# Wider spacing between wo's loads and their splits, and scratch matmuls among seven of v's products

## The chip, the core and the metric

The kernel runs on one core of a Trainium2 chip. The metric is the device time of one execution in microseconds (us). The core has five engines that work through their own queues and wait for each other by semaphores: TensorE (PE, matrix products, with its weight loads shown apart as PEld), VectorE (DVE), ScalarE (ACT), GpSimd (POOL) and SyncE (SP, which here issues DMA transfers). A kernel is compared with another by the medians of several runs.

## The reference

The input x has 2048 rows of 512. Two branches work on it and are mixed by a gate per row. The reference, cut to what is computed:

```python
def _A_ref(x, wq, wk, wv, wo):              # 32 heads of 16, one k and one v for all
    q = (x @ wq).reshape(B, S, H, Dh).transpose(0, 2, 1, 3)
    k, v = x @ wk, x @ wv
    p = softmax(einsum("bhqd,bkd->bhqk", q, k) * Dh ** -0.5)
    o = einsum("bhqk,bkd->bhqd", p, v)
    return o.transpose(0, 2, 1, 3).reshape(B, S, H * Dh) @ wo

def _B_ref(x, w1, b1, w2, b2):              # 512 -> 1792 -> 512
    h = relu(x @ w1 + b1)
    return (h * h) @ w2 + b2

g = sigmoid((x * gate_w).sum(-1, keepdims=True))
return g * _A_ref(x, ...) + (1 - g) * _B_ref(x, ...)
```

## The kernel before

**Precision.** The larger products (those of q, the dense branch and the output) run on numbers that are split in two: a rounded part r and the rest l = value - r. Each product is then three matmuls (r with r, r with l, l with r). `split` makes the two parts on DVE: a CAST (line 192) and a subtraction (line 193). The weights wo are split once, in four quarters, into wor and wol.

**Attention.** The 32 heads and four chunks of 512 query rows make 32 iterations. In each, 32 steps u (units of key tile and half chunk) run through: scores on PE (line 763) go either into the two-bank tiles s, from which ACT takes the exponential straight into e (line 800), or into the single bank x, which DVE copies to e first (line 784, COPY e<-x), so that ACT takes the exponential there. Then PE multiplies e with v into the accumulator acc (line 814, the context, groups of 16 or 24 matmuls in the profile). At an iteration's end the accumulator is copied, repacked by DMA (oc, lc) and divided on DVE (lines 833 to 840). The bank x is one only: PE's next score in x waits for DVE's copy of the one before.

**Other matmuls.** Between the scores of a block stand the twelve-matmul units of the projections of q, the dense branch and the output projection. They come from the generator `work` and accumulate in the banks mm (line 1107). Every 32 x 512 block of scores and its unit of matmuls form a "phase", followed by a context block.

**The order of the work.** It is laid out by a planner in the kernel's own Python. It keeps estimated times of the engines, at_pe, at_act and at_dve. Work of DVE that has no fixed place stands in lists: `soon`, `divisions`, `chores`. `spend` takes from them whatever fits until the given estimated time, divisions ahead of chores, chores in order. A chore that loads something returns a number of microseconds, and `held` is then set to that much after the present estimate: the next chore that computes is placed no earlier. The number is LANDS (6.0) or DIVIDES (10.0) us. The tile `stage` takes what is loaded so: its first half serves the chores (wo here, later x and the attention's output), its other two quarters belong to the loads of w1 and w2. wo is loaded in two transfers of two quarters each (line 943), and each transfer is followed in `chores` by two splits.

**The start.** v comes as sixteen small products of 17 columns (`v_tiles`, line 336) out of kvc, into a bank vp that is later called acc. After each of the first nine stands a scratch matmul (line 339) into columns of the same bank that nobody reads: 240 columns wide, with the constant ones as weights. The last seven stand behind the first scores; behind them come a tiny copy named peek (line 1208), which makes DVE pass a finished bank, the copies of v and z (`v_rows`, lines 343 and 344) and a row of k_aug (`k_shift`, line 330).

**SP's queue** issues, in order, the loads of weights (line 474), of wo (943), of b2 (1033), the writes and reads of q's parts in DRAM (355, 420, 434) and the repacking (204, 205). A transfer that waits holds up those behind it.

Of the kernel before, what the change touches and what calls it, by code (L numbers as in the profile page):

```python
# [32 lines left out]
ROOT = float(0x1fbd1df5 + 0x80000)  # L33
WARM = 10
PARTS = [slice(a, min(a + 86, CH)) for a in range(0, CH, 86)]
LANDS, DIVIDES, SURE = 6.0, 10.0, 0.7
PAIR, CONTEXT, TURN, EXP, COPY, LATE = 0.235, 0.429, 0.36, 0.925, 0.66, 0.3
GROUPS = (0, 1, 2, 3), (4, 5, 6, 7), (8, 9, 10), (11, 12, 13)
AHEAD = 4
# [124 lines left out]
def mix_kernel(ctx: ExitStack, tc: tile.TileContext, xT, wkv, wq, wo, w12, b1, b2, cst, out):  # L164
# [63 lines left out]
    with fast, tc.tile_pool(name="at", bufs=1) as at, \  # L228
# [103 lines left out]
        def v_tiles(tiles, vp, idle=0):  # L332

            for i in tiles:
                c, j = divmod(i, 4)
                nc.tensor.matmul(vp[:, i * 17:i * 17 + 17], kvc[:, c, j * 128:(j + 1) * 128],
                                 cs[:, C_SEL:C_SEL + 17], start=True, stop=True)
                for _ in range(idle):
                    nc.tensor.matmul(vp[:, 272:], ones, sqk[:, 0, 272:], start=True, stop=True)

        def v_rows(vp):
            vz = vp[:, :16 * 17].rearrange("p (i d) -> p i d", i=16)
            nc.vector.tensor_copy(v_ext[:, :, 0:32:2], vz[:, :, :DH])
            nc.vector.tensor_copy(z, vz[:, :, DH])
# [96 lines left out]
        def stage():  # L441

            if not staged:
                staged.append(keep.tile(sh, F32, name="stage", tag="r2"))
            return staged[0]
# [136 lines left out]
        vp = ap.tile([128, CH], F32, name="acc")  # L582
# [26 lines left out]
        def later(f, *args):  # L609
            chores.append((1.2, lambda: f(*args)))  # L610
# [326 lines left out]
        def o_ready(c):  # L937

            if c == 0 and not wos:
                wos.extend(xp.tile(sh, F32R, name=n, tag=t) for n, t in (("wor", "xr2"), ("wol", "xl2")))  # L940

                def load(a):
                    nc.sync.dma_start(stage()[:, :2], wo[a * 256:a * 256 + 256].rearrange("(t p) n -> p t n", p=128))
                    return LANDS

                for t in range(KT):
                    if t % 2 == 0:
                        chores.append((0.0, lambda t=t: load(t // 2)))
                    later(split, wos[0][:, t], wos[1][:, t], stage()[:, t % 2])
            if c > 0:  # L950
                ask(c - 1)

        def ask(c, n=KT):
            if c in asked or any((c, t) not in complete for t in range(n)) or c > len(asked):
                return
            if c and not used[c - 1]:
                return
            asked.add(c)
            tiles = []

            def load(a):
                if a == 0:
                    tiles.extend((keep.tile(sh, F32R, name="orr", tag="r3"), xp.tile(sh, F32R, name="orl", tag="xl3")))
                m = min(2, n - 2 * a)
                i = c * NG + 4 * a
                nc.sync.dma_start(stage()[:, :m], oTs[i:i + 2 * m].rearrange("(t u) d n -> (u d) t n", u=2))
                return DIVIDES

            def part(t):
                orr, orl = tiles  # L970
                split(orr[:, t], orl[:, t], stage()[:, t % 2])
                if t == n - 1:
                    osp[c] = orr, orl

            for t in range(n):
                if t % 2 == 0:
                    chores.append((0.0, lambda t=t: load(t // 2)))
                later(part, t)
# [228 lines left out]
        phase(span.slots, AHEAD + 2, 0)  # L1207
        nc.vector.tensor_copy(at.tile([128, 1], F32, name="peek"), span.bank[:, :1])
        evicted = True
        v_tiles(range(9, 16), vp)  # L1210
        v_rows(vp)
        k_shift(1)
        dve(1.6, at_pe + 2.2)
# [72 lines left out]
```

## Time and profile before

| | |
|---|---|
| median of 3 runs | 1226.75 us (1225.81 to 1229.14) |
| profiled execution | 1228.71 us, of which its span 1227.0 us |
| mean granted TensorE clock | 0.994 |
| busy: PE, ACT, DVE, weight loads, POOL | 99%, 84%, 63%, 55%, 5% of the span |
| the chain of waits by line | PE acc L814 37%, PE mm L1107 33%, PE s L763 17%, PE x L763 6% |

The span is the time from the first to the last instruction of the profiled execution. The granted clock is the share of full speed that TensorE's throttle allowed. A busy share says how long an engine had work, not that it set the time; the chain of waits is followed back from the last instruction to what released each step, and says whose work the end hung on. Idle time of PE shows in the timeline in brackets, with what ended it.

### The profile page before, as it was taken

The page shows a single profiled execution, that of the slowest core. Times are in us where ns is not written, and L with a number is a line of the kernel's source. Part 1 is how long each engine was busy: PE and PEld are TensorE (multiplying, and loading weights), DVE is VectorE, ACT ScalarE, POOL GpSimd, SP SyncE. Part 2 cuts the span into 40 slices and gives each one's busy share as a digit, 9 for nine tenths or more (in the row PEclk, how much of TensorE's full clock was granted, in tenths as well). Part 3 has the DMA queues.
Part 4 walks back from the last instruction along what each step waited for, and adds up shares of the span by engine and source line. Part 5 has one row for each costly group of instructions (what it writes and reads, how often), then busy time and mean ns, then how long its engine had stood idle before and what let it go on. Part 6 is the DMA issues. An engine that isn't in the chain of part 4 may idle for free.

```text
span 1227.0 us, 24104 instructions
## 1 busy us (share of the span) xinstructions
PE 1211.2 (99%) x9839; PEld 673.4 (55%) x9839; DVE 771.2 (63%) x1516; ACT 1035.5 (84%) x1146; POOL 66.3 (5%) x87
## 2 busy tenths in 40 slices
PE   9999989999999999999999999999999999999997
PEld 4555545555555555555555555555555555555553
DVE  5765768466576864837678574655848476663643
ACT  6788868888988888888888888988888888988875
POOL 1001020000000200000002001000010000001000
PEclk9999989999999999999999999999999999999999
DMA  6344331121113223112133122112132222113011
GB/s 227 78 120 117 102 88 49 48 75 40 52 57 120 88 74 91 53 32 66 57 100 117 57 61 92 49 40 74 38 91 64 57 67 81 36 31 91 23 52 37
DMA packets 45347, 88.71 MB, mean 72 GB/s; under 512 B 10642, under 2 KB 10898, under 8 KB 44720
## 3 DMA queue, kind: packets, MB, share of 16 engines
q1 hardware_dynamic: 37024, 68.27, 18.7%
q0 software_dynamic: 8064, 18.59, 4.9%
q8 instruction: 79, 1.29, 0.5%
q14 instruction: 36, 0.29, 0.1%
q10 hardware_dynamic: 144, 0.26, 0.1%
HBM read 57.83 MB, written 20.97 MB: 64 GB/s over the span
## 4 chain that ended last, share of the span: by engine, by line
PE 93%; DVE 2%; ACT 2%; DMA 1%; SPq 1%; issue 1%; DVEq 0%; ACTq 0%
PE acc L814 37%; PE mm L1107 33%; PE s L763 17%; PE x L763 6%; ACT e L800 1%; DVE e L784 1%; SPq L420 1%; DMA stage<-in_wo 0%; DMA xf<-in_xT 0%; PE mm L296 0%; PE mm L200 0%; DVE qr L392 0%; DVE ql L393 0%; PE s L306 0%; DVE ot L1249 0%
## 5 line engine op out<-in xcount | busy, mean ns | idle before, releaser
L800 ACT ACTIVATE e<-s 128x1024 f32<-128x1024 f32 x822 | 781.7, 1026 | 165.9 <-PE s L763 165.3
L784 DVE COPY e<-x 128x512 f32<-128x512 f32 x404 | 279.1, 691 | 389.1 <-PE x L763 354.1
L814 PE MATMUL acc<-e,v_ext 128*32 128x512 f32 (+1 forms) x4224 | 484.3, 586 | 0.0
L763 PE MATMUL s<-qa,k_aug 49*128 49x512 f32 x1644 | 462.4, 413 | 0.2
L763 PEld LDWEIGHTS s<-qa,k_aug 49*128 49x128 f32 x1644 | 234.8, 185 | 75.0 <-ACT e L800 54.0
L814 PEld LDWEIGHTS acc<-e,v_ext 128*32 128x32 f32 x4224 | 116.1, 109 | 241.9 <-issue 238.2
L1107 PE MATMUL mm<-w2r,hr 64*128 64x512 f32 x896 | 229.2, 402 | 0.0
L800 ACT ACTIVATE e<-e 128x1024 f32<-128x1024 f32 x202 | 214.7, 1063 | 0.8 <-DVE e L784 0.8
L763 PE MATMUL x<-qa,k_aug 49*128 49x512 f32 x404 | 164.7, 408 | 5.4 <-DVE e L784 4.2
L1107 PEld LDWEIGHTS mm<-w2r,hr 64*128 64x128 f32 x896 | 135.7, 186 | 45.9 <-DVE hr L193 9.2
L1107 PE MATMUL mm<-w2l,hr 64*128 64x512 f32 x448 | 143.9, 392 | 0.0
L763 PEld LDWEIGHTS x<-qa,k_aug 49*128 49x128 f32 x404 | 75.1, 186 | 51.3 <-DVE w2l L491 12.6
L1107 PEld LDWEIGHTS mm<-w2l,hr 64*128 64x128 f32 x448 | 80.5, 186 | 6.9
L1107 PE MATMUL mm<-xragain,w1r 64*128 64x512 f32 x224 | 76.3, 418 | 0.2
L1107 PE MATMUL mm<-xr,w1r 64*128 64x512 f32 x224 | 74.3, 416 | 0.0
L1107 PE MATMUL mm<-xlagain,w1r 64*128 64x512 f32 x224 | 74.0, 391 | 0.0
L1107 PE MATMUL mm<-xragain,w1l 64*128 64x512 f32 x224 | 73.1, 392 | 0.0
L1107 PE MATMUL mm<-xl,w1r 64*128 64x512 f32 x224 | 72.4, 391 | 0.0
L1107 PE MATMUL mm<-xr,w1l 64*128 64x512 f32 x224 | 72.0, 395 | 0.0
L839 DVE RECIPROCAL n<-n 128x86 f32<-128x86 f32 x90 | 61.5, 683 | 1.8
L1107 PEld LDWEIGHTS mm<-xragain,w1r 64*128 64x128 f32 x224 | 38.2, 185 | 27.7 <-issue 9.2
L1107 PEld LDWEIGHTS mm<-xr,w1r 64*128 64x128 f32 x224 | 37.9, 185 | 26.8 <-issue 8.4
(162 smaller groups left out, 1181.4 us busy)
## 6 DMA issues: line engine op xcount, KB each, us to landing
stage<-in_w SPq DMA_DIRECT2D x56, 256.0 KB
qa<-qs SPq DMA_DIRECT2D x186, 64.0 KB
w1f<-in_w SPq DMA_DIRECT2D x28, 256.0 KB
w2f<-in_w SPq DMA_DIRECT2D x28, 256.0 KB
qs<-qr SPq DMA_DIRECT2D x16, 256.0 KB
ress<-res POOLq DMA_DIRECT2D x4, 1024.0 KB, 5.1
qs<-ql POOLq DMA_DIRECT2D x15, 256.0 KB, 7.5
oc<-accs SPq DMA_DIRECT2D x30, 128.0 KB
```

The costliest lines, as they stand in the source:

```text
L420: nc.sync.dma_start(bass.AP(tensor=o.tensor, offset=o.offset, ap=[[KS * 2 * CH, 4], [CH, 2], [1, CH]]), nrm[32 * i:32 * i + 8].bitcast(F32))
L763: nc.tensor.matmul(dst.rearrange("p (a n) -> p a n", a=2), k_aug[rows, kt * 128:(kt + 1) * 128], qa[it][rows, :, q * HC:q * HC + HC], star ...
L784: nc.vector.tensor_copy(e_half(u)[:, 2 * r:2 * r + 2], x.rearrange("p (a n) -> p a n", a=2))
L800: nc.scalar.activation(e_half(u), src, AF.Exp, scale=SCALE)
L814: nc.tensor.matmul(acc[h * 32:(h + 1) * 32, cols], v_ext[:, kt], es[u // 2][:, h % 2 * 2 + h // 2, mine], start=(kt == 0), stop=(kt == NK ...
L839: return ((0.23, bound), (0.35, compare), (0.72, lambda: nc.vector.reciprocal(n[0], n[0])), (0.28, lambda: nc.vector.tensor_tensor(o[:, co ...
L1107: nc.tensor.matmul((self.before if r else self).bank, a[p], b[p], start=not r and i == 0, stop=r == 1 and i == len(self.terms[1]) - 1, ski ...
```

## The change

A new constant, WRITES = 14.0, is what a load of wo returns in place of LANDS = 6.0. And the last seven products of v get one scratch matmul each, as the first nine have. They are 240 columns wide; the constant ones is their weight.

```diff
-LANDS, DIVIDES, SURE = 6.0, 10.0, 0.7
+LANDS, DIVIDES, WRITES, SURE = 6.0, 10.0, 14.0, 0.7
...
                 def load(a):
                     nc.sync.dma_start(stage()[:, :2], wo[a * 256:a * 256 + 256].rearrange("(t p) n -> p t n", p=128))
-                    return LANDS
+                    return WRITES
...
         evicted = True
-        v_tiles(range(9, 16), vp)
+        v_tiles(range(9, 16), vp, 1)
         v_rows(vp)
         k_shift(1)
```

The first number moves instructions on DVE and on SP's queue. PE's, ACT's and POOL's orders stay as they are but for the scratch matmuls.

On DVE, around the first two splits of wo, at 168.56 and 170.24 us of the profile, the order before is:

```order
L784 COPY e<-x 128x2x256
L491 TENSOR_TENSOR w1l<-stage,w1r 128x512
L784 COPY e<-x 128x2x256
L192 CAST wor<-stage 128x512
L193 TENSOR_TENSOR wol<-stage,wor 128x512
L784 COPY e_1883<-x 128x2x256
L192 CAST wor<-stage 128x512
L193 TENSOR_TENSOR wol<-stage,wor 128x512
L784 COPY e_1883<-x 128x2x256
L662 TENSOR_SCALAR big<-mm,b1t 128x512
```

The same place of DVE now:

```order
L784 COPY e<-x 128x2x256
L784 COPY e_1888<-x 128x2x256 x2
L662 TENSOR_SCALAR big<-mm,b1t 128x512
L663 TENSOR_TENSOR big<-big 128x512
L192 CAST hr<-big 128x512
L193 TENSOR_TENSOR hr<-big,hr 128x512
L784 COPY e<-x 128x2x256 x2
L482 CAST w1r<-w1f 128x512
L491 TENSOR_TENSOR w1l<-w1f,w1r 128x512
L784 COPY e<-x 128x2x256
L192 CAST wor<-stage 128x512
L193 TENSOR_TENSOR wol<-stage,wor 128x512
```

The two pairs CAST and TENSOR_TENSOR on wo have left this place; the first pair of the new order stands where the third stood before (181.18 us), the second where the fourth stood (190.00 us).

The third and fourth pairs now stand on DVE behind the divisions of the next finished pair of iterations, which before ended at 216.00 us:

```order
L839 RECIPROCAL n<-n 128x82
L784 COPY e<-x 128x2x256
L840 TENSOR_TENSOR oc<-oc,n 128x82
L192 CAST wor<-stage 128x512
L193 TENSOR_TENSOR wol<-stage,wor 128x512
L784 COPY e<-x 128x2x256
L686 SCALAR_TENSOR_TENSOR res_2133<-mm,omg,res_2133 128x512
L192 CAST wor<-stage 128x512
L193 TENSOR_TENSOR wol<-stage,wor 128x512
```

Before, there was no work on wo at this place; the other rows stood in the same order.

On SP's queue the second load of wo moves behind eleven transfers (a load of w1, the two of the repacking, eight of q for the next iteration):

```order
 L474 DMA stage<-in_w 128x512
+L474 DMA w1f<-in_w 128x512
+L204 DMA oc<-accs 64x512
+L205 DMA lc<-accs 64x512
+L434 DMA qa<-qs 16x1024 x3
+L434 DMA qa<-qs 1x1024
+L434 DMA qa<-qs 16x1024 x3
+L434 DMA qa<-qs 1x1024
 L943 DMA stage<-in_wo 128x2x512
-L474 DMA w1f<-in_w 128x512
```

The first load keeps its place.

On PE, among the last seven products of v:

```order
 L763 MATMUL s<-qa,k_aug 128x512 x2
-L336 MATMUL acc<-cs,kvc 128x17 x7
+L336 MATMUL acc<-cs,kvc 128x17
+L339 LDWEIGHTS ones
+L339 MATMUL acc<-sqk,ones 128x240
+L336 MATMUL acc<-cs,kvc 128x17
```

The last three rows repeat until there are seven products and seven scratch matmuls.

## The prediction

> **What bounds the kernel now.** I read the page's chain of waits first, to learn which engine sets the end.
>
> ```profile
> PE 93%; DVE 2%; ACT 2%; DMA 1%; SPq 1%; issue 1%; DVEq 0%; ACTq 0%
> ```
>
> TensorE (PE) carries 93% of the chain, so a microsecond counts only if PE loses it. I then listed the granted clock in half-microsecond stretches over the whole span. Apart from the last four microseconds, after PE's work, it is below full in only two places, around 32 to 36 us and 168 to 176 us. The windows view over both places (length, then busy us and, in brackets, instructions of PE, its weight loads, DVE, ACT and POOL, then the granted clock, the DMA share and GB/s):
>
> ```profile
> 21.96:25.38 3.42, 3.34 (x31) 2.83 (x30) 2.80 (x8) 3.00 (x6) 0.00 (x0) 1.00 0.44 99
> ...
> 28.79:32.20 3.41, 3.41 (x25) 2.46 (x21) 2.65 (x7) 3.02 (x4) 0.00 (x0) 1.00 0.17 60
> 32.20:35.61 3.41, 3.26 (x17) 2.60 (x18) 3.27 (x10) 2.99 (x3) 0.00 (x0) 0.50 0.74 231
> ...
> 165.25:168.66 3.41, 1.68 (x15) 1.03 (x11) 0.10 (x1) 1.96 (x2) 0.00 (x0) 1.00 0.83 304
> 168.66:172.07 3.41, 1.70 (x9) 0.96 (x13) 3.34 (x7) 0.00 (x0) 2.66 (x2) 0.51 0.04 11
> 172.07:175.49 3.42, 3.42 (x16) 0.47 (x16) 2.75 (x4) 1.97 (x2) 3.42 (x3) 0.50 0.59 153
> ```
>
> The clock is halved for 3.41 us and later for 6.83 us, twice that; and from 35.61 to 168.66 there are 39 times 3.41 us. So in this trace the clock is set anew every 3.41 us on a fixed beat: a stretch in which PE did too little is followed by one at half speed. Each part of the change stands in the stretch ahead of one of these two drops. The timeline (start, duration, engine, operation; in brackets the idle time before it and what ended it) shows the second place on VectorE (DVE) and PE:
>
> ```profile
> 168.56 0.43 DVE L192 CAST wor<-stage 128x512 fp32r<-128x512 f32 x1 [5.34 <-DMA stage<-in_wo]
> ...
> 169.63 0.68 DVE L784 COPY e<-x 128x512 f32<-128x512 f32 x1
> ```
>
> ```profile
> 162.96 1.92 PE L814 MATMUL acc<-e,v_ext 128*32 128x512 f32 x16
> ...
> 170.37 0.79 PE L763 MATMUL x<-qa,k_aug 49*128 49x512 f32 x1 [3.44 <-DVE e L784]
> ...
> 171.95 3.64 PE L814 MATMUL acc<-e,v_ext 128*32 128x512 f32 x16
> 175.52 0.52 PE L1107 MATMUL mm<-xr,w1r 64*128 64x512 f32 x2
> ...
> 178.12 1.92 PE L814 MATMUL acc<-e,v_ext 128*32 128x512 f32 x16
> ```
>
> DVE stands 5.34 us at the first split of wo, whose load has not landed. The copy of scores behind it, which empties the one bank x, is late, and PE, which needs x, stands 3.44 us. Then PE works at half clock until 175.5 us: the same sixteen context matmuls take 3.64 us there and 1.92 elsewhere. The chain of waits, in order of time, gives the landing, and the starts of undisturbed context blocks:
>
> ```profile
> 163.31 5.24 DMA stage<-in_wo
> ...
> 178.17 1.87 PE acc L814 x16
> 182.58 1.85 PE acc L814 x16
> 187.00 1.85 PE acc L814 x16
> ```
>
> **The change part by part.** First, the splits. The order shows no change in PE's, ACT's or POOL's work from here on. On DVE, two pairs leave the place of 168.56 and 170.24; the next two places, which served the second load, now serve the first; and two new places follow behind the divisions. What the first load then meets:
>
> ```profile
> 181.18 0.42 DVE L192 CAST wor<-stage 128x512 fp32r<-128x512 f32 x1
> ```
>
> Without the stall this place is reached some 6.3 us sooner, at about 174.9 us, and the load lands at 163.31 + 5.24 = 168.55: 6.3 us to spare. If PE is also earlier by the second part below, so is the load's issue, which follows PE and DVE. What that saves: from the context block at 162.96 to the one at 178.12 are 15.16 us for two periods (each sixteen context matmuls, two x products, six s products and twelve of the unit). Undisturbed periods of this form take 182.58 - 178.17 = 4.41 and 187.00 - 182.58 = 4.42 us. So the loss here is 15.16 - 8.83 = **6.3 us**: 3.44 of standing, half of the 5.15 us from 170.37 to 175.52 for the clock, and 0.3 around them. Its lower bound is 3.44 us, if the clock dropped all the same.
>
> The second load moves on SP's queue (the DMA queue of SyncE) from its old place ahead of the second row here to one ahead of the last, behind eleven others:
>
> ```profile
> 156.59 6.68 SPq L420 DMA_DIRECT2D qs<-nrm  x4
> ...
> 179.75 0.33 SPq L474 DMA_DIRECT2D w1f<-in_w  x1
> ...
> 191.01 3.38 SPq L434 DMA_DIRECT2D qa<-qs  x8
> 194.48 0.35 SPq L474 DMA_DIRECT2D stage<-in_w  x1
> ```
>
> It is issued where the last row stands, less the 7.5 us by which all is earlier here: about 187 us, and lands, by the first load's 5.24, near 192. The weights' load of the last row goes out 0.4 us later behind it; its reader comes 12 us after the issue, which hides that:
>
> ```profile
> 206.93 0.63 ACT L496 ACTIVATE w1r<-stage 128x512 fp32r<-128x512 f32 x1
> ```
>
> The new places of the splits are behind the rows of 216.00 and 219.07 on DVE:
>
> ```profile
> 216.00 0.23 DVE L840 TENSOR_TENSOR oc<-oc,n 128x82 f32<-128x82 f32 x1
> 218.47 0.69 DVE L784 COPY e<-x 128x512 f32<-128x512 f32 x1 [2.23 <-PE x L763]
> 219.07 0.74 DVE L686 SCALAR_TENSOR_TENSOR res<-mm,omg,res 128x512 f32<-128x512 f32 x1
> 222.60 0.69 DVE L784 COPY e<-x 128x512 f32<-128x512 f32 x1 [2.79 <-PE x L763]
> ```
>
> They come up near 208.7 and 212.3 us, over 16 us behind the landing. A pair takes 169.63 - 168.56 = 1.07 us and falls into DVE's idle 2.23 and 2.79 us: no cost. Without that cover each would hold up a copy of x, 1.1 us apiece. The finished halves of wo are first read much later, so nobody else waits for them:
>
> ```profile
> L1107 PE MATMUL mm<-wor,orr x120: 385/394/502, 459.8 to 1203.5; 64*128 64x512 f32 x120
> ```
>
> Second, the scratch matmuls. Seven products of v are now each followed by a matmul of 240 columns, as the first nine were already:
>
> ```profile
> 24.50 0.30 PE L336 MATMUL acc<-cs,kvc 128*128 128x17 f32 x2
> ...
> 24.75 0.30 PE L336 MATMUL acc<-cs,kvc 128*128 128x17 f32 x2
> ...
> 29.82 1.74 PE L336 MATMUL acc<-cs,kvc 128*128 128x17 f32 x14
> ```
>
> With scratch a product takes 24.75 - 24.50 = 0.25 us. Without, fourteen halves take 1.74 us, of which the last 0.26 is one duration: 1.48 / 13 x 2 = 0.23. So seven scratch matmuls add 7 x 0.02 and the last one's end, 0.25 us together. PE then has a wait that covers it:
>
> ```profile
> 32.16 0.15 DVE L1208 COPY peek<-mm 128x1 f32<-128x1 f32 x1
> ...
> 32.36 0.28 PEld L1107 LDWEIGHTS mm<-xr,wqr 64*128 64x128 f32 x1 [0.59 <-DVE peek L1208]
> ...
> 32.74 0.87 DVE L330 TENSOR_SCALAR k_aug<-km 1x512 fp32r<-1x512 f32 x2
> ...
> 33.24 1.01 ACT L800 ACTIVATE e<-s 128x1024 f32<-128x1024 f32 x1
> ...
> 36.28 0.39 PE L1107 MATMUL mm<-xr,wql 64*128 64x512 f32 x1
> 36.51 0.39 PE L1107 MATMUL mm<-xr,wqr 64*128 64x512 f32 x1
> ...
> 37.52 2.78 PE L814 MATMUL acc<-e,v_ext 128*32 128x512 f32 x24
> ```
>
> The peek does not depend on v, so PE goes on at 32.37 as before; 0.25 us is the price if that wait were gone. Does the clock hold? The stretch 21.96 to 25.38 held all nine products with scratch and was followed by full clock; the stretch 28.79 to 32.20 held the seven bare ones, with PE busy throughout by the page, and was followed by half. In the new order the latter gets 7 x 240 columns more, so I take it that the clock holds. What that is worth: PE's steps after 32.37 at full clock come every 0.23 us (36.28 to 36.51). Three steps, and the score pair stands at about 33.1; but its second half needs the shifted row of k_aug, ready at 32.74 + 0.87 = 33.61, so PE leaves it at 33.7, where it is today. Three steps and a score pair: 34.6. Three steps: 35.3; the next score pair needs the bank that ACT frees with the end of the activation after that of 33.24, 33.24 + 2 x 1.01 = 35.3: no wait to speak of. The pair and three steps, and context begins near 36.3 instead of 37.52: **1.2 us**. The bounds are nothing (the clock drops anyway) and half of the 3.41 us, 1.7.
>
> [...]
>
> **The sum** is made against the profiled execution, 1228.71 us (its span 1227.0, and 1.7 around it): 1228.71 - 6.3 - 1.2 = **1221.2 us**. That execution is 1.96 above the median 1226.75, and the runs go from 1225.81 to 1229.14. I read the spread as the fixed beat falling elsewhere: were a stretch to begin just ahead of PE's standing, one half-clock stretch would follow, not two, and at the first place perhaps none. With the drops gone the new kernel should have little of this spread, so I put its median at 1221.2, and not at 1226.75 - 7.5 = 1219.2, which stays the lower bound. To 1226.75 that is -5.5 us, 0.45%.
>
> **The rivals.**
>
> The clock falls at 32 us regardless, because what counts is the wait for the peek or a measure of work that 240 columns do not reach. For it: the beat's place differs by run. Against: the stretch 21.96 to 25.38. [...] Price: the second term lost, 1222.4.
>
> The wait moves rather than goes: the first split still waits, or a split on its new place holds a copy of x. For it: SP's queue took 6.68 us for four small issues (qs<-nrm) just ahead of the first load, and may take longer. Against: 6.3 and 16 us to spare. Half a stall, say 2 us of standing and a half-clock stretch of 3.41 us (1.7): 1225.
>
> Slower: the second load stays stuck behind the eight loads of q and the third split stands. It holds DVE, x and so PE, as at 168.56. It costs from the point at which the load lands after 208.7 us, against 192 expected. It decides once the new kernel loses 1230.4 - 1221.2 = 9.2 us (0.3% above the old median), that is 6.6 us of standing and 2.6 of half clock: a landing past 215.3 us; at 216 the time is 1231. The hold-up of 6.7 us in the SP rows above is what speaks for it; 23 us of it is far off.
>
> **How the numbers follow.** Forecast 0.79, own range 1219.2 to 1222.2; clock falls anyway 0.10; wait moves 0.08; slower 0.03. The measurement tells about 0.3%, 3.7 us, from no change: faster means below 1223.1. The forecast and the first rival lie below it, 0.89 together, the wait that moves lies within, and the slower case is above. The range for 8 in 10 takes in the lower bound with 0.4 us beneath it for the runs' own scatter, and the first rival with half of the second: 1218.8 to 1224.0.
>
> **What would show it.** On the changed kernel's timeline, no idle time ahead of a split of wo; x at about 165.7 us copied by DVE without delay; context blocks 4.4 us apart through 160 to 180; the granted clock 1.00 in all stretches until PE's last work; context first at 36.3. A clock of 0.5 at 32 refutes the second term; a DVE row on wor released by stage<-in_wo refutes the first. If both are as said and the time is above 1223, something outside these two places took it back.

## The result and the profile after

| | before | changed |
|---|---|---|
| median, runs beside each other | 1226.38 us (1225.09 to 1229.14, 7 runs) | 1221.62 us (1220.89 to 1222.54, 7 runs) |
| profiled execution, and its span | 1228.71 us, 1227.0 us | 1221.62 us, 1219.9 us |
| mean granted TensorE clock | 0.994 | 0.999 |

The ratio is 0.9952, with a 95% interval of 0.9937 to 0.9966: the changed kernel is faster by 0.48%. The forecast was 1221.2 us.

The page of the changed kernel, the chain of waits by engine:

```profile
PE 94%; DVE 2%; ACT 2%; DMA 1%; issue 1%; SPq 0%; ACTq 0%; DVEq 0%
```

PE carries a little more of a shorter chain (94% against 93%), so part of what went was time in which PE did not work; work at half clock counts as PE's share all the same (3.57 us of acc at 172.02 in the chain of before, against 1.85 to 1.87 for a block at full clock). The windows view of the changed kernel over two stretches of its own beat at the start, and over the place of the old stall (window, its length, then busy us and instructions of PE, its weight loads, DVE, ACT and POOL, granted clock, DMA share, GB/s):

```profile
29.19:32.60 3.41, 3.41 (x30) 2.59 (x30) 2.80 (x8) 2.94 (x5) 0.00 (x0) 1.00 0.15 54
32.60:36.01 3.41, 3.35 (x29) 2.32 (x25) 3.03 (x7) 3.41 (x5) 0.00 (x0) 1.00 0.75 246
160.00:167.00 7.00, 7.00 (x60) 3.63 (x60) 3.87 (x6) 6.43 (x7) 1.10 (x1) 1.00 0.44 153
167.00:176.00 9.00, 9.00 (x76) 4.61 (x72) 7.57 (x13) 7.70 (x9) 5.40 (x4) 1.00 0.10 29
```

Both drops of the clock are gone, and PE is busy for all 16 us of 160 to 176. (The edges of the beat are counted back in steps of 3.413 us from the drop behind PE's last work. The step is measured in before: 307 of them lie between the end of the half clock at 175.59 us and the drop at 1223.48, and 39 between 35.64 and 168.76.) The timeline of the changed kernel on DVE, where the four splits of wo stand now:

```profile
164.13 0.69 DVE L784 COPY e<-x 128x512 f32<-128x512 f32 x1 [1.83 <-PE x L763]
...
173.81 0.42 DVE L192 CAST wor<-stage 128x512 fp32r<-128x512 f32 x1
...
182.62 0.42 DVE L192 CAST wor<-stage 128x512 fp32r<-128x512 f32 x1
...
208.75 0.42 DVE L192 CAST wor<-stage 128x512 fp32r<-128x512 f32 x1
...
212.33 0.42 DVE L192 CAST wor<-stage 128x512 fp32r<-128x512 f32 x1
```

No split has a bracket, so none waits; the copy of x waits for PE, and no longer the other way round. On PE, the first context block, and those through the old stall:

```profile
36.28 1.92 PE L814 MATMUL acc<-e,v_ext 128*32 128x512 f32 x16
...
161.74 1.92 PE L814 MATMUL acc<-e,v_ext 128*32 128x512 f32 x16
...
166.14 1.92 PE L814 MATMUL acc<-e,v_ext 128*32 128x512 f32 x16
...
170.75 1.92 PE L814 MATMUL acc<-e,v_ext 128*32 128x512 f32 x16
```

They are 4.40 and 4.61 us apart, at 1.92 us each: 9.01 us for the two periods that took 15.16. And SP's queue in the changed kernel:

```profile
153.39 3.85 SPq L420 DMA_DIRECT2D qs<-nrm  x4
157.29 0.44 SPq L943 DMA_DIRECT2D stage<-in_wo  x1
...
183.63 3.38 SPq L434 DMA_DIRECT2D qa<-qs  x8
187.10 0.39 SPq L943 DMA_DIRECT2D stage<-in_wo  x1
```

The first load goes out 6 us sooner than in the profile of before; only 1.2 us of that is the lead that all had by then.

Where the 7.1 us between the two spans lie is read from the starts of context blocks in both traces, before less changed: 1.24 us at the first (37.52 and 36.28), 1.22 at the block of 82.92 and 81.70, 0.87 at the next, 1.22 again at 162.96 and 161.74, 7.37 behind the old stall (178.12 and 170.75), 7.10 at the end. The 0.35 us at 87 us is a wait that is new on DVE:

```profile
83.86 0.43 DVE L482 CAST w1r<-w1f 128x512 fp32r<-128x512 f32 x1 [1.27 <-DMA w1f<-in_w]
```

Its load was issued at 80.58, behind q's eight loads, against 79.40 before. Three more steps of about 0.3 us, at 267, 464 and 659 us, are given back by 958 us. They stand in the profiles of after_again, after_more, narrow32, long_peek, writes10, filled_stall and only_scratch too, and not in those of only_writes and before_2, which lack the seven scratch matmuls. act_queue, which has them, shows the step at 267 and little of the other two. What makes the steps is not known.

### The profile page after: what moved, and what is told of

Its sections match the earlier page's. It is cut to its first block, busy times and chain, and to the rows that moved or that the text cites. A ratio compares the mean times of both kernels' runs of the same rounds, so it can differ in the third digit from the quotient of the medians.

```text
span 1219.9 us, 24119 instructions
## 1 busy us (share of the span) xinstructions
PE 1207.6 (99%) x9845; PEld 669.9 (55%) x9846; DVE 771.5 (63%) x1516; ACT 1035.1 (85%) x1146; POOL 64.8 (5%) x87
## 4 chain that ended last, share of the span: by engine, by line
PE 94%; DVE 2%; ACT 2%; DMA 1%; issue 1%; SPq 0%; ACTq 0%; DVEq 0%
PE acc L814 37%; PE mm L1107 33%; PE s L763 17%; PE x L763 6%; ACT e L800 2%; DVE e L784 1%; DMA xf<-in_xT 0%; PE mm L296 0%; PE mm L200 0%; DMA w1f<-in_w 0%; DVE qr L392 0%; DVE ql L393 0%; PE s L306 0%; DVE ot L1249 0%; PE x L881 0%
```

## The experiments

Four questions: does each part do what it was credited with; why was the load late; what makes the clock fall; and where do the runs of the kernel before get their spread. None of the kernels leaves out work of the reference.

### Each part alone, and the change once more

only_writes takes the scratch matmuls out of the changed kernel:

```diff
-        v_tiles(range(9, 16), vp, 1)
+        v_tiles(range(9, 16), vp)
```

> The wider spacing of wo alone, v's last seven products bare. Theory (two separate losses, of which the stall of DVE and PE at the first split is one): no wait on stage<-in_wo, context blocks 4.4 us apart at 160 to 180 us, the clock at 0.5 for one stretch of 3.4 us near 32 us, first context block near 37.5 us; median 1222.4 to 1223.0. Rival (the scratch matmuls did nothing, all of the gain is the spacing's): 1221.6.

Measured: 1222.62 us (1221.81 to 1226.59, 11 runs), ratio 0.9975 (0.9961 to 0.9989). The windows view of only_writes over two stretches of its beat:

```profile
29.61:33.02 3.41, 3.22 (x25) 2.61 (x25) 2.62 (x8) 2.94 (x4) 0.00 (x0) 1.00 0.25 66
33.02:36.43 3.41, 3.41 (x19) 2.85 (x17) 2.57 (x5) 3.02 (x4) 0.00 (x0) 0.50 0.72 243
```

The drop at the start is there, the first context at 37.46, and no split waits. The splits' part alone does what was said of it.

only_scratch takes the splits' part out:

```diff
-                    return WRITES
+                    return LANDS
```

> The seven scratch matmuls alone, wo's splits where they were. Theory: first context block near 36.3 us, full clock there; the first split of wo waits 3 to 5 us and the clock falls after it; median 1225.2, 1.2 below before. Rival 1 (scratch did nothing): 1226.4. Rival 2 (the earlier start lets SP's queue issue wo's load sooner, as it did in the changed kernel, 157.3 against 163.3 us, so the stall shrinks by itself): 1221.6 to 1223.

Measured: 1227.48 us (1223.47 to 1232.08, 12 runs), ratio 0.9998 (0.9981 to 1.0015), some 2 us above what was expected. The first context stands at 36.38, so the start was repaired. The stall took that back. DVE's timeline in only_scratch, and then the step of its chain of waits behind it:

```profile
168.50 0.43 DVE L192 CAST wor<-stage 128x512 fp32r<-128x512 f32 x1 [5.87 <-DMA stage<-in_wo]
```

```profile
159.24 9.24 DMA stage<-in_wo
```

The load went out 4.1 us sooner than in the profile of before (163.31) and landed at the same 168.5, after 9.24 us in place of 5.24. The lead of 1.1 us at the start was lost in the longer wait. As a measure of the scratch alone this run is inconclusive: the stall's own spread is wider than 1.2 us.

after_again is the changed kernel without any edit, run beside these.

> The changed kernel once more, beside the two halves on the same chip. 1221.6, with a profile whose context blocks start within 0.4 us of the first profile's; where they differ, in steps of 0.3 us, the steps are scatter and not the change's.

Measured: 1221.38 us (1220.99 to 1221.93, 6 runs), ratio 0.9952 (0.9938 to 0.9966). Less only_writes, 1222.62, that prices the scratch at 1.24 us.

### Why the load was late

act_queue keeps the splits where they were before and sends wo's loads through ScalarE's queue (the scratch matmuls stay):

```diff
-                    nc.sync.dma_start(stage()[:, :2], wo[a * 256:a * 256 + 256].rearrange("(t p) n -> p t n", p=128))
-                    return WRITES
+                    nc.scalar.dma_start(stage()[:, :2], wo[a * 256:a * 256 + 256].rearrange("(t p) n -> p t n", p=128))
+                    return LANDS
```

> The scratch matmuls, wo's splits where they were before (6.0 us of spacing), but wo's two loads are issued from ACT's queue instead of SP's. Theory A (the load was late because it stood behind q's small writes on SP's queue, 6.7 us): it goes out some 5 us sooner, lands before the split's place, no stall, 1221.3 to 1222.3. Theory B (6.0 us is too short for the transfer itself, wherever it is issued): DVE waits 2 to 5 us again, 1224 to 1225.5.

Measured: 1221.85 us (1220.68 to 1222.68, 6 runs), ratio 0.9953 (0.9938 to 0.9968). The timeline of act_queue: the load's issue on ScalarE's queue, and the first split.

```profile
155.45 0.42 ACTq L943 DMA_DIRECT2D stage<-in_wo  x1
```

```profile
163.23 0.42 DVE L192 CAST wor<-stage 128x512 fp32r<-128x512 f32 x1
```

The split is at its old place and waits for nothing: the load was there by 163.23. It went out 0.93 us ahead of SP's first issue of qs<-nrm, which stands at 156.38 in this trace. So the load was late because of what stood ahead of it in SP's queue, and spacing the splits is one of two cures that are equal within the scatter.

The traces in which a split waits say more. In each, the start of the four qs<-nrm (the timeline of SP), the load's issue, and its landing (from the chain of waits; in filled_stall, from the split that it releases):

| | q's eight loads | qs<-nrm begins | wo issued | wo landed | from qs<-nrm |
|---|---|---|---|---|---|
| before | 7.87 us | 156.59 | 163.31 | 168.55 | 11.96 |
| before_2 | 6.59 us | 155.74 | 159.88 | 167.97 | 12.23 |
| only_scratch | 7.21 us | 156.23 | 159.24 | 168.48 | 12.25 |
| filled_stall (below) | 5.32 us | 153.21 | 157.00 | 165.6 | 12.4 |
| writes10 (next) | 8.38 us | 156.34 | 162.18 | 167.72 | 11.38 |
| before_3 (below) | 7.38 us | 161.56 | 164.59 | 174.01 | 12.45 |
| only_scratch_2 (below) | 7.80 us | 161.19 | 167.93 | 173.28 | 12.09 |

The issue moves by 3.7 us (3.01 to 6.74) against the start of the writes (2.96 to 6.69 us of them) and the landing hardly: the load comes about 12 us after the first of the four writes, however soon it is issued behind them. The hold-up is thus not the queue's issuing alone. It fits a load that stands behind the writes' data, but that was not tried by itself. A lack of bandwidth does not fit in before_2: the DMA share, taken each half microsecond from 165.0 to 167.5, was 0.24 to 0.31, while the load was still out (it landed at 167.97). In before it was 0.80 to 1.04 from 165 to 168, with the load out until 168.55, so there it is not ruled out. And the writes in turn begin 0.8 to 1.4 us after q's eight loads ahead of them have been issued. The timeline of SP in filled_stall, where those took 5.32 us:

```profile
146.54 5.32 SPq L434 DMA_DIRECT2D qa<-qs  x8
...
153.21 3.74 SPq L420 DMA_DIRECT2D qs<-nrm  x4
157.00 0.44 SPq L951 DMA_DIRECT2D stage<-in_wo  x1
```

In before they took 7.87 us from 147.74 on. So in these traces the landing is spread, against PE's work, mostly by how long SP is busy with q's loads, two steps ahead.

writes10 sets the constant to 10.0, between the two:

```diff
-LANDS, DIVIDES, WRITES, SURE = 6.0, 10.0, 14.0, 0.7
+LANDS, DIVIDES, WRITES, SURE = 6.0, 10.0, 10.0, 0.7
```

> The changed kernel with 10.0 in place of 14.0: the first split stands one copy later than before, some 2.5 us on in time, and the third ahead of one place less. Theory (the stall is as long as the load lands after the split's place): with landings seen between 162 and 168.5 us the wait is 2.5 us shorter and often gone, median 1221.5 to 1223.5, the scatter between that of before and that of the changed kernel. Rival (any place past the planner's 6 us will do): 1221.4, no scatter.

Measured: 1223.93 us (1222.12 to 1228.74, 12 runs), ratio 0.9977 (0.9963 to 0.9991), some 0.4 us above what the theory expected and far from the rival's. The timeline of writes10, DVE and then PE:

```profile
167.74 0.43 DVE L192 CAST wor<-stage 128x512 fp32r<-128x512 f32 x1 [2.59 <-DMA stage<-in_wo]
```

```profile
170.21 0.50 PE L1107 MATMUL mm<-xr,w1r 64*128 64x512 f32 x2 [1.82 <-DVE big L662]
...
173.10 0.50 PE L763 MATMUL x<-qa,k_aug 49*128 49x512 f32 x1 [0.53 <-DVE e L784]
```

The split waits 2.59 us, half of what it did, and what stands behind it on DVE is late: first line 662, which empties a bank mm that PE waits 1.82 us for, then a copy of x, 0.53 us. The clock does not fall: the context blocks at 173.76 and 178.14 take 1.92 us each, and the mean clock of this execution is 0.999. The gain follows the spacing: some 2 to 2.5 us are still lost at 10 (against 1221.38 and 1221.93 for the unedited kernel, run beside other experiments), none at 14.

### What the stall costs beside the wait

filled_stall keeps the old places and puts fourteen matmuls of 512 columns on PE where it stands, into a bank of s that is overwritten afterwards (LANDS in place of WRITES, as in only_scratch, and this, which the first split of wo sets off):

```diff
+                for _ in range(fill.pop()):
+                    nc.tensor.matmul(parts[u + 1][0][:, 0], cs[:, :64].bitcast(BF), cs[:, :CH // 2].bitcast(BF),
+                                     start=True, stop=True)
             score(u, r, x)
```

> Scratch among v's products, wo's splits at their old place, and 14 scratch matmuls of 512 columns (3.0 us) on PE ahead of the product x that waits in the stall: the wait stays, the clock should not fall. Theory (of the stall's 6.3 us, 3.4 are standing and 2.6 the half clock behind it): full clock at 165 to 180 us, and from the block ahead of the wait to the one after the next 8.8 us plus the standing alone, some 12.3 instead of 15.2; median 2 to 2.6 below the scratch alone, 1224 to 1225.5. Rival (the loss is the standing and its backlog on DVE, the clock is by the way): as the scratch alone, 1227.

Measured: 1225.84 us (1224.79 to 1231.04, 12 runs), ratio 0.9991 (0.9974 to 1.0007). The timeline of filled_stall, DVE and then PE:

```profile
165.59 0.43 DVE L192 CAST wor<-stage 128x512 fp32r<-128x512 f32 x1 [3.47 <-DMA stage<-in_wo]
```

```profile
165.47 3.19 PE L786 MATMUL s<-cs 128*128 128x512 bf16 x13
...
168.59 0.50 PE L763 MATMUL x<-qa,k_aug 49*128 49x512 f32 x1
```

PE has work through the wait and the clock stays at full: the context blocks behind it, at 169.49 and 174.08, take 1.92 us each. The median is 1.6 us under that of only_scratch, 2 to 2.6 were expected, and the two ranges and the intervals of the two ratios overlap: the direction is as the theory has it, but by the times alone it is not clear of the noise. The clock is: 11 of the 12 runs have a mean clock of 0.998 or more, against 4 of only_scratch's 12. (Its single wait of 3.47 us is no measure of the edit: the writes began 3 us earlier in this execution.) So PE at work through this stall kept the clock (0.999 over the profiled execution); the wait stayed.

### What makes the clock fall at the start

narrow32 makes the seven scratch matmuls 32 columns wide (`v_tiles` passes the width on to line 339):

```diff
-        v_tiles(range(9, 16), vp, 1)
+        v_tiles(range(9, 16), vp, 1, 32)
```

> The changed kernel, with the seven new scratch matmuls cut from 240 to 32 columns. Theory (the clock is set by the columns that PE streams in a stretch of 3.4 us): 32 columns are too little, the clock is at 0.5 for one stretch near 32 to 36 us, first context block near 37.4 us, median 1222.4 to 1222.8, as with bare products. Rival (any further matmul between the products holds the clock, whatever its width): clock 1.00, context near 36.4, 1221.4.

Measured: 1222.28 us (1221.65 to 1223.92, 9 runs), ratio 0.9962 (0.9946 to 0.9978). In the profiled execution the clock stays full and the first context stands at 36.47, against what was expected. The median lies between that of the changed kernel and that of only_writes. The runs beside the profiled one differ from it: the four at a mean clock of 0.999 go from 1221.65 to 1222.17 us, the five at 0.998 or less from 1222.28 to 1223.92. Of only_writes' 11 runs ten are at 0.998 or less, of the changed kernel's 25 (counted further down) one. So by the mean clock 32 columns hold it in some runs and not in others.

long_peek puts a reduction, estimated at 0.7 us, on DVE ahead of the peek, which makes PE's wait longer (0.93 us against 0.35), with all of the change in place:

```diff
         phase(span.slots, AHEAD + 2, 0)
+        nc.vector.tensor_reduce(at.tile([128, 1], F32, name="slow"), span.bank, AX.X, OP.max)
         nc.vector.tensor_copy(at.tile([128, 1], F32, name="peek"), span.bank[:, :1])
```

> The changed kernel with one more reduction of 0.7 us on DVE ahead of the peek, so that PE waits there about 1.0 us instead of 0.35, longer than the 0.59 of the kernel before. Theory (thin matmuls set off the drop, not this wait): full clock, first context block 0.3 to 0.7 us later than in the changed kernel, 1221.7 to 1222.1. Rival (the wait for the peek sets it off): 0.5 for 3.4 us, context 1.5 us and more later, 1222.9 or above.

Measured: 1222.13 us (1221.41 to 1226.46, 8 runs), ratio 0.9963 (0.9943 to 0.9982). The timeline of PE's weight loads in long_peek shows the longer wait, and the windows view what followed:

```profile
33.24 0.18 PEld L1107 LDWEIGHTS mm<-xr,wqr 64*128 64x128 f32 x1 [0.93 <-DVE peek L1209]
```

```profile
30.22:33.64 3.42, 2.92 (x28) 2.32 (x30) 2.68 (x8) 2.94 (x5) 0.00 (x0) 1.00 0.27 77
33.64:37.05 3.41, 3.41 (x20) 2.67 (x18) 2.96 (x6) 2.15 (x3) 0.00 (x0) 0.50 0.75 226
```

With scratch in place and a wait of 0.93 us the drop is back in this execution: 1.00 becomes 0.50 at the edge of the beat behind it. It is not so in most runs: six of the eight have a mean clock of 0.999 or more and lie from 1221.41 to 1222.74 us, about where the theory had them. So with the longer wait the drop comes in some runs only, by the mean clock; that the beat's place is the reason is the author's guess, which no run shows.

### Where the spread of the runs comes from

The experiments up to here suggested that the landing of the load alone, and not the beat, might spread the runs of the kernel before. Two more profiled executions of that kernel (before_2, before_3), and one more of only_scratch (only_scratch_2), were to tell the two apart.

> The kernel before once more, for where its scatter comes from. Theory A: the landing of wo's first load sets it, through SP's queue and the transfer; the profiled time then follows the idle time that the trace shows ahead of the first split of wo: 5.34 us of it went with 1228.71, and each microsecond less of idle time should take 1 to 1.4 us off, down to 1222.6 with no idle time. Theory B (the prediction's): the fixed beat of the clock falls elsewhere; then the idle time ahead of the split is again 5 to 5.6 us, and the time differs by the number of half-clock stretches, 1.7 us each.

> A third look at the kernel before. Theory A: time and idle time ahead of the first split of wo move together as in the run beside it. Theory B: the idle time stays at 5 to 5.6 us and the time follows the number of half-clock stretches.

> The kernel with the scratch matmuls alone, once more. Theory A: its profiled time is 1221.5 us and 1 to 1.4 us for each microsecond of idle time ahead of the first split of wo (5.87 us went with 1228.95). Theory B: idle time near 5.9 us again, and a time that differs by 1.7 us for each half-clock stretch more or less.

Measured, one profiled execution each: 1227.13, 1233.54 and 1233.19 us. The wait ahead of the first split, on DVE's timeline of before_2:

```profile
167.99 0.43 DVE L192 CAST wor<-stage 128x512 fp32r<-128x512 f32 x1 [5.84 <-DMA stage<-in_wo]
```

and of only_scratch_2:

```profile
173.30 0.43 DVE L192 CAST wor<-stage 128x512 fp32r<-128x512 f32 x1 [5.47 <-DMA stage<-in_wo]
```

In before_3 it was 6.69 us. These waits differ by little from the 5.34 and 5.87 of the earlier profiles, while the times differ by 6 us. only_scratch_2 refutes theory A: by it a wait of 5.47 goes with 1227 to 1229 us. The clock tells them apart. The windows view of before_2 over its beat, at the start and at the stall:

```profile
30.28:33.69 3.41, 3.22 (x25) 2.56 (x26) 2.61 (x7) 2.94 (x5) 0.00 (x0) 1.00 0.34 92
33.69:37.11 3.42, 3.36 (x29) 1.85 (x29) 2.71 (x5) 3.36 (x4) 0.00 (x0) 1.00 0.66 204
...
166.82:170.23 3.41, 0.43 (x4) 0.39 (x5) 2.17 (x5) 0.00 (x0) 1.39 (x1) 1.00 0.11 42
170.23:173.64 3.41, 3.41 (x21) 0.73 (x17) 3.32 (x5) 1.97 (x2) 3.41 (x3) 0.50 0.30 113
```

No drop at the start, with bare products, and one stretch at half speed behind the stall. The same view of only_scratch_2:

```profile
22.53:25.94 3.41, 3.27 (x28) 2.60 (x29) 2.79 (x7) 2.26 (x5) 0.00 (x0) 1.00 0.60 160
25.94:39.59 13.65, 13.65 (x61) 10.74 (x60) 8.69 (x19) 8.63 (x9) 0.00 (x0) 0.50 0.32 105
```

Here, as in before_3, the clock falls at 26 us, ahead of the seven products, and stays at half for four beats. The first contexts stand at 41.58 (before_3) and 41.52 (only_scratch_2), 5.2 us late; in only_scratch_2 seven scratch matmuls did not help. Half-clock stretches ahead of PE's end: 3 in the first profile of before (1228.71 us), 1 in before_2 (1227.13), 6 in before_3 (1233.54), 2 in only_scratch (1228.95), 5 in only_scratch_2 (1233.19). The time follows their number, at 1.7 us each, and PE's standing together, which was 3.44, 3.95, 4.79, 4.27 and 3.87 us, to within 3 us: a half-clock stretch in which PE stands anyway costs less (in before_3 PE is busy for only 0.54 us of the one from 172.98 on).

The mean clock of each run says the same of many. Over the 69 runs of the kernel before that stood beside the experiments, it and the time have a correlation of -0.83; the 15 runs at 0.999 or more have a median of 1223.82 us, the 26 at 0.996 or less one of 1228.73. But those 15 still go from 1222.21 to 1225.74: what is left there is probably the standing, which varies with the landing: the writes ahead of the load begin between 153.2 and 156.6 us in the profiles above whose start was not delayed.

after_more is the changed kernel again, for the drop at 26 us:

> The changed kernel again, for more runs. In two traces, one of the kernel before and one with the scratch matmuls alone, the clock fell already at 26 us, ahead of the seven products, and stayed at half for four beats, 13.65 us, which put the first context 5.2 us later. The change does not touch that place. Theory A: this strikes the changed kernel as it does the others, in about one run of nine; then among some ten runs one or so is near 1226 us at a mean clock of 0.994, and the rest lie from 1220.7 to 1222.7. Theory B: the changed kernel is free of it, and all runs lie from 1220.7 to 1222.7.

Measured: 1221.93 us (1221.04 to 1222.78, 12 runs), ratio 0.9959 (0.9946 to 0.9972), every run at a clock of 0.998 or more. With after and after_again that makes 25 runs of the changed kernel, up to 1222.78 us, without the drop at 26. Of the 69 runs of before, at most 6 had it, by a mean clock of 0.994 or less; at that rate 25 clean runs come up one time in ten (63/69 to the power of 25). So the runs lean to theory B, but do not show it, and nothing in the change, which does not touch that place, would be a reason for it. Kernels with the same seven scratch matmuls speak against it: writes10, which differs in the constant alone, had one run of 12 at 0.993 (1228.74 us), and long_peek one of 8 at 0.994 (1226.46). Neither was profiled, so that the drop at 26 is behind them is not shown. It stays open.

No version was found that is faster than the changed kernel; act_queue equals it.

## Why the prediction was right

**The bound, and the beat.** Right. Only time that PE lost counted. The beat of 3.41 us holds in each trace in which two edges far apart were read: 307 steps from 175.59 to 1223.48 us in before, 309 from 170.23 to 1224.94 in before_2, 43 from 26.20 to 172.98 in before_3, 44 from 25.94 to 176.12 in only_scratch_2. The long drop of 13.65 us is four of it.

**The stall, put at 6.3 us.** Right in mechanism and, on the profile, in size: the two periods shrank from 15.16 to 9.01 us, 6.15. Its make-up of standing and clock is borne out by filled_stall, where with PE at work through the wait the clock was at full (0.998 or more in 11 of 12 runs) and the wait of 3.47 us remained, and by act_queue, where a load that comes in time gives back all of it, with the splits unmoved. As a typical figure it is large. From the medians the splits' part is worth 1226.71 - 1222.62 = 4.1 us, since other runs have a shorter stall.

**The new places.** 173.81, 208.75 and 212.33 us, against 173.7 (174.9 less the 1.2 of the second part), 208.7 and 212.3; the second load issued at 187.10 against 187. No cost, as said.

**The scratch, put at 1.2 us and at no price of its own.** Right on the profile (first context at 36.28 against 36.3) and between kernels (1.24). PE's timeline in the changed kernel, among the seven products, and then that of its weight loads, with the wait behind them:

```profile
29.95 0.26 PE L339 MATMUL acc<-sqk,ones 96*128 96x240 bf16 x1
30.05 0.30 PE L336 MATMUL acc<-cs,kvc 128*128 128x17 f32 x2
30.19 0.26 PE L339 MATMUL acc<-sqk,ones 96*128 96x240 bf16 x1
```

```profile
32.27 0.18 PEld L1107 LDWEIGHTS mm<-xr,wqr 64*128 64x128 f32 x1 [0.35 <-DVE peek L1208]
```

A scratch matmul comes every 0.24 us and a product between each two. The wait for the peek shrank from 0.59 to 0.35 us, 0.24 of the 0.25 that scratch takes, so it was the cover. The 0.35 us at 87 us were not foreseen.

**Why the clock fell.** Here the reason was too simple. The prediction blamed the thin products, by one stretch with scratch that held and one without that fell, and kept the wait for the peek as a rival at 0.10. The stretches around 30 us, by kernel, with the wait that PE's weight loads show:

| stretch of the beat | kernel | scratch | wait for the peek | next stretch |
|---|---|---|---|---|
| 28.82 to 32.23 | before | none | 0.59 | half |
| 29.19 to 32.60 | changed | 240 | 0.35 | full |
| 29.45 to 32.86 | act_queue | 240 | 0.34 | full |
| 29.61 to 33.02 | only_writes | none | 0.62 | half |
| 30.22 to 33.64 | long_peek | 240 | 0.93 | half |
| 30.28 to 33.69 | before_2 | none | 0.61 | full |
| 30.31 to 33.72 | after_again | 240 | 0.36 | full |
| 30.36 to 33.78 | narrow32 | 32 | 0.44 | full |

Where the stretch holds all seven products (the first four rows), bare ones were followed by the drop and those with scratch were not, with edges so close that the beat's place is no excuse: the changed kernel's and act_queue's lie between those of before and only_writes. only_scratch and filled_stall, with scratch, held as well: their first contexts stand at 36.38 and 36.07. But in the first four rows scratch and a shorter wait, 0.35 in place of 0.6 us, come together, so they do not tell the two causes apart. Where the stretch begins among the products, bare ones passed as well (before_2, with a wait of 0.61), so narrow32's profile proves nothing about 32 columns; and there the drop came even with scratch where the wait was 0.93 (long_peek).

Standing was read where the matmuls are wide, too. In writes10 PE was busy for only 1.59 of the 3.41 us from 167.12 on, with 1.82 us of standing, and in only_scratch_2 for 1.95 from 169.29 on; the clock stayed at full in the stretch behind each. It fell behind 1.58 us (before, from 165.35 on). So in those two stretches 1.82 and 1.46 us without work brought no drop, while ahead of the drops at the start PE was busy for 2.92 to 3.40 us (long_peek, only_writes, before) and waited for 0.59 to 0.93. That thin products count for little is the author's reading of this; that with 240 columns behind each the clock held at this place in seven of nine profiles (long_peek fell behind it, only_scratch_2 ahead of it), and with 32 in some runs, fits it but does not show it. So the prediction's reason is neither refuted nor shown, and the rival may be right in part: long_peek fell with scratch in place and a wait of 0.93 us. How products and wait weigh against each other, and what the beat's place adds, no run shows; nor was the measure found by which the work of a stretch decides the clock of the next.

That the beat's place differs by run, as the prediction's first rival had it, is borne out: the edges lie at 28.82, 29.62 (before_3, counted back) and 30.28 us in three profiles of one kernel.

**The sum and the median.** 1221.2 forecast against a median of 1221.62; the profiles differ by 7.1 us where 7.5 was worked out. The choice not to take 7.5 off the median was right: the kernel before had that profile's loss in some runs and less in others. The cause given for the spread, the beat falling elsewhere, is borne out by before_2, which has the very case that the prediction named (no drop at the start, one stretch behind the stall). What was left out is that the standing spreads too, with the landing. On the means of 69 and 25 runs the change gains 1226.94 - 1221.73 = 5.2 us; half of 3.41 us for each half-clock stretch is in the mean clock, 0.9969 against 0.9993, which makes 3.8 - 0.9 = 2.9 us of it. So at most somewhat over half of the gain is clock and the rest standing: the mean clock also counts half-clock time in which PE stands, 1.6 us of it in the profile of before (168.76 to 170.37), which is already counted as standing.

**The rivals.** The wait that moves and the slower case did not come: the second load went out 21 us ahead of its reader's place. The signs named for each step came out as said, but for one period of 4.61 us among those of 4.4.

## What to carry to other kernels

When a load is late, look at what its queue carries ahead of it: here it landed about 12 us after four small writes began, however soon it was issued behind them, and going ahead of them on another queue cured the wait as well as 8 us more of spacing did. A stall of PE is priced with the clock behind it, here 1.7 us for each half-clock stretch of full work (half of 3.41), and such a stretch can come although PE looks busy: before fell behind one with PE busy for 3.40 of 3.41 us, which held thin matmuls, with a wait of 0.59 at its end. And one profile is one draw: the edges of the beat lay at 28.82, 29.62 and 30.28 us in three profiles of one kernel, and their times went from 1227.13 to 1233.54. So read the spread of the runs and the mean clock of each before taking a profile's loss off the median.

## What was not expected of the hardware

- The clock fell at 26 us for 13.65 us in two of three further profiles, although PE was busy for 3.27 of the 3.41 us of the stretch ahead. only_writes had a stretch at nearly the same place with the same busy times, and held. Its windows view:

```profile
22.78:26.19 3.41, 3.27 (x29) 2.60 (x28) 2.79 (x7) 2.07 (x4) 0.00 (x0) 1.00 0.59 169
```

No quantity in these views tells it from the 22.53 to 25.94 of only_scratch_2. In before_3, which fell, the stretch lay from 22.79 to 26.20, with PE and its weight loads busy for the same 3.27 and 2.60 us. No run here settles what tells them apart.

- An earlier issue did not bring an earlier landing. Behind the same four writes, the load of wo took 9.24 us when they were issued in 2.96 us (only_scratch) and 5.24 when they took 6.68 (before). What it waits for behind them was not tried.
- A scratch matmul of 32 columns between two products took the same place as one of 240: the products stay 0.25 us apart.
